# Fused attention and MLP layer: VectorE's exp tiles taken eight units ahead, more zero matmuls, and a one-quad first PV

## The chip, the cores and the metric

The kernel runs on one core of a Trainium2 chip. The metric is the device time of one execution in microseconds (us); lower is better. Each time here is a median of several executions. "Clock" is the mean granted clock of TensorE (PE) over an execution, 1.00 being full speed. ACT is ScalarE, DVE is VectorE.

## The reference, cut to what matters

```python
# x: (1, 2048, 640) bf16; 32 heads of 20; MLP width 1728
def _A_ref(x, wqkv, wo):
    q, k, v = ...                                   # split of x @ wqkv by head
    scores = jnp.einsum("bhqd,bhkd->bhqk", q, k) * (Dh ** -0.5)
    p = _softmax(scores, axis=-1)
    o = jnp.einsum("bhqk,bhkd->bhqd", p, v)
    return o.transpose(...).reshape(B, S, D) @ wo
h  = x + _A_ref(_layernorm(x), wqkv, wo)
h2 = h + _B_ref(_layernorm(h), w_gate, w_up, w_down)   # gelu(g) * u, then down
```

The attention has 32 x 2048 x 2048 exponentials. They are most of the work of this kernel.

## The kernel before

The kernel is written as a list of operations with priorities. A list scheduler inside the kernel, with its own table of durations, fixes each engine's program order when the kernel is built; the chip then runs these fixed orders with semaphores.

Words used below:

- A **tile** is 128 partitions by 512 columns of scores, for one head. The heads of a group of four are numbered j = 0 to 3, and head j's q and k lie in partitions 32j to 32j+31. Its score matmuls use only 32 rows of PE.
- A **unit** is three or two consecutive tiles; ACT takes their exp in one instruction of 1536 or 1024 columns. Units alternate between PSUM banks 0-2 and 3-4, so the scores of a unit can start when the exp two units earlier has freed its banks.
- A **group** (a "slot" in the code) is 64 tiles, about 22 units. Eight of its tiles (two in the first group) go to DVE, which computes exp in integer and bf16 arithmetic, two tiles at a time.
- **PV** multiplies finished probabilities with V, one **quad** (four heads) at a time. It frees the probability buffer, a ring of 18 tiles.
- The queries are handled in seven **chunks** (numbered 0 to 6, of 512, 512, 256, 256, 256, 128 and 128); output projection, LayerNorm and MLP of a finished chunk run as background work among the next chunk's attention. What is left of it after the last exp, with the last chunk's own part, is the **tail**.

How tiles are given out, before: DVE's tile is the next in the sequence after its unit, and its scores are issued right behind the unit's.

```python
        while i < len(tiles):                      # (cut)
            units.append(tiles[i:i + len(bs)])     # 3 or 2 tiles with consecutive j
            i += len(units[-1])
            want = min(nd, (k[0] - D_FIRST) * nd // D_SPAN + 1) if k[0] >= D_FIRST else 0
            if k[1] < want and tiles[i][0] == s_:
                dtile.append(tiles[i])             # the next tile: the next j
                i += 1                             # (cut)
```

```python
                return lambda eng: eng.matmul(out()[:, kk * nq:(kk + 1) * nq],       # scores, tile (s_, g, kb, j)
                                              kt_all[32 * j:32 * j + 32, g, kt * 128:(kt + 1) * 128],
                                              qt_all[32 * j:32 * j + 32, q0 // 512, g, q0 % 512:q0 % 512 + nq],
                                              start=True, stop=True, tile_position=(32 * j, 0), skip_group_check=True)
```

Padding: before it places a PV operation, the scheduler looks at how busy PE was in the last 3.4 us of its model, and adds groups of four zero matmuls (added to the output bank, so without effect) until a threshold is met. With nothing else to do, it places "warming" work (a full-size matmul, or a group of four zero ones) by a second threshold.

```python
                    while u < PAD_MIN * PAD_WIN and o.util < 1.1:
                        o.fns = o.fns + self.pad       # four zero matmuls, one per column group
                        o.dur += 0.215
```

## Time and profile before

The median is 928.82 us (three runs, 928.81 to 929.91).

| | read in | value |
|---|---|---|
| busy share of ACT | busy table | 95% |
| first exp starts, last exp ends | timeline of ACT | 35.74, 890.21 us |
| first to last exp ("the stream") | difference | 854.47 us |
| last exp to end ("the tail") | span less 890.21 | 37.15 us |
| exp of 1536 / 1024 columns, start to start | start times of the exps, median | 1.331 / 0.904 us |

The head of the page of the kernel before, with busy time and share by engine:

```profile
span 927.4 us, 23141 instructions
PE 837.1 (90%) x10069; PEld 356.9 (38%) x10126; DVE 811.3 (87%) x1703; ACT 883.2 (95%) x799; POOL 39.1 (4%) x117
```

Groups of the page: busy us and mean ns of one, then the engine's idle time ahead of them and what ended it. They are the scores, the two exp groups (ACT writes into either of two buffers) and the zero matmuls. Each exp group holds both widths, half of each, though its line names only 1536 columns.

```profile
L852 PE MATMUL ps<-qt_all,kt_all 32*128 32x256 bf16 (+2 forms) x3584 | 304.9, 289 | 51.2 <-ACT pts L339 29.1
L339 ACT ACTIVATE pts<-ps 128x1536 bf16<-128x1536 f32 x480 | 571.7, 1368 | 5.1 <-PE ps L852 3.8
L339 ACT ACTIVATE rege<-ps 128x1536 bf16<-128x1536 f32 x239 | 298.8, 1367 | 2.4 <-PE ps L339 1.5
L339 PE MATMUL ps<-kt_all,zer 128*32 128x512 bf16 x680 | 56.4, 384 | 0.0
```

ACT is idle only 7.5 us ahead of all 719 exps, and half of that is the first one. Note the 1368 ns: an exp is recorded longer than the mean spacing of exps, because successive records overlap. The Trainium skill ("Perfetto Trace Analysis", Per-instruction lifecycle) says that an ACT record runs on to the write's acknowledgement; this trace agrees, with 1.58 us recorded for 1536 columns against a spacing of 1.331. So the idle column misses delays shorter than the overlap, and I measure an exp's **delay** by start times: start to start, less the median of its width (1.331 or 0.904 us). Delays of at most 0.25 us I call **short**, the others **long** (pairs with a table load between them are left out). Before, the short ones sum to 6.6 us and the long ones to 7.0.

The tail in ACT's timeline (start, duration, group, and in brackets idle time and what ended it):

```profile
888.62 1.59 ACT L339 ACTIVATE rege<-ps 128x1536 bf16<-128x1536 f32 x1
890.23 1.28 ACT L339 ACT_TABLE_LOAD   x1
891.52 0.20 ACT L339 ACTIVATE nm<-off 128x1 f32<-128x1 f32 x1
896.02 0.70 ACT L567 ACTIVATE rege<-ps 128x640 bf16<-128x640 bf16 x1 [4.29 <-PE ps L561]
```

And PE's timeline there. The last scores are at 888.06; then come 25 down-projection matmuls of an older chunk (L1096), and the last PV starts at 891.89, 1.7 us after the last exp:

```profile
888.06 0.40 PE L852 MATMUL ps<-qt_all,kt_all 32*128 32x128 bf16 x12
888.39 3.57 PE L1096 MATMUL ps<-regw,rege 128*128 128x320 bf16 x25
891.89 0.45 PE L339 MATMUL ps<-pts,v_all 128*21 128x128 bf16 x17
```

### The profile page before, as it was taken

The page shows a single profiled execution, that of the slowest core. Times are in us where ns is not written, and L with a number is a line of the kernel's source. Part 1 is how long each engine was busy: PE and PEld are TensorE (multiplying, and loading weights), DVE is VectorE, ACT ScalarE, POOL GpSimd, SP SyncE. Part 2 cuts the span into 40 slices and gives each one's busy share as a digit, 9 for nine tenths or more (in the row PEclk, how much of TensorE's full clock was granted, in tenths as well). Part 3 has the DMA queues.
Part 4 walks back from the last instruction along what each step waited for, and adds up shares of the span by engine and source line. Part 5 has one row for each costly group of instructions (what it writes and reads, how often), then busy time and mean ns, then how long its engine had stood idle before and what let it go on. Part 6 is the DMA issues. An engine that isn't in the chain of part 4 may idle for free.

```text
span 927.4 us, 23141 instructions
## 1 busy us (share of the span) xinstructions
PE 837.1 (90%) x10069; PEld 356.9 (38%) x10126; DVE 811.3 (87%) x1703; ACT 883.2 (95%) x799; POOL 39.1 (4%) x117
## 2 busy tenths in 40 slices
PE   3998999899998998998797898999899998989998
PEld 2432322222232222233233333344345455546677
DVE  8859999999898998888798997988998997899972
ACT  6899999999999999999999999999999999999951
POOL 5000000000001000000001000000200200010100
PEclk9999999999999999999999999999999999999999
DMA  7301010322540000001021000011000100101000
GB/s 256 94 19 43 18 55 18 90 60 66 155 176 18 12 1 1 1 15 44 1 31 23 8 2 1 16 30 31 16 16 2 23 23 2 31 17 24 3 24 16
DMA packets 39517, 34.36 MB, mean 37 GB/s; under 512 B 19436, under 2 KB 36936, under 8 KB 39416
## 3 DMA queue, kind: packets, MB, share of 16 engines
q1 hardware_dynamic: 39416, 32.89, 12.7%
q8 instruction: 79, 1.29, 0.6%
q14 instruction: 22, 0.18, 0.1%
HBM read 20.12 MB, written 8.09 MB: 30 GB/s over the span
## 4 chain that ended last, share of the span: by engine, by line
ACT 73%; PE 14%; DVE 9%; DMA 2%; POOL 1%; issue 1%; SPq 0%
ACT pts L339 46%; ACT rege L339 25%; PE ps L1039 3%; PE ps L616 3%; DVE qt_all L339 3%; PE ps L1096 3%; PE ps L852 3%; PE ps L339 2%; DVE rege L339 2%; DMA regw<-in_A_wqkv_dram 1%; ACT L339 1%; DVE rege L812 1%; DVE qt_all L812 1%; POOL nw L339 0%; PE ps L561 0%
## 5 line engine op out<-in xcount | busy, mean ns | idle before, releaser
L339 ACT ACTIVATE pts<-ps 128x1536 bf16<-128x1536 f32 x480 | 571.7, 1368 | 5.1 <-PE ps L852 3.8
L852 PE MATMUL ps<-qt_all,kt_all 32*128 32x256 bf16 (+2 forms) x3584 | 304.9, 289 | 51.2 <-ACT pts L339 29.1
L339 ACT ACTIVATE rege<-ps 128x1536 bf16<-128x1536 f32 x239 | 298.8, 1367 | 2.4 <-PE ps L339 1.5
L852 PEld LDWEIGHTS ps<-qt_all,kt_all 32*128 32x128 bf16 x3584 | 96.4, 92 | 279.8 <-ACT pts L339 160.0
L339 DVE TENSOR_TENSOR qt_all<-qt_all 128x1024 bf16<-128x1024 bf16 (+1 forms) x240 | 164.4, 685 | 3.7
L1039 PE MATMUL ps<-rege,regw 128*128 128x256 bf16 (+2 forms) x957 | 149.2, 287 | 10.3 <-ACT rege L339 2.8
L339 PE MATMUL ps<-pts,v_all 128*21 128x256 bf16 (+2 forms) x2098 | 138.8, 290 | 1.0 <-DVE rege L339 1.0
L812 DVE TENSOR_SCALAR rege<-ps 128x512 int16<-128x512 f32 x154 | 105.3, 684 | 23.9 <-PE ps L852 23.1
L339 DVE TENSOR_SCALAR qt_all<-qt_all 128x1024 bf16<-128x1024 int16 (+1 forms) x288 | 115.8, 417 | 2.4
L339 PE MATMUL ps<-rege,v_all 128*21 128x256 bf16 (+2 forms) x1294 | 113.3, 292 | 0.1
L1039 PEld LDWEIGHTS ps<-rege,regw 128*128 128x128 bf16 x980 | 72.0, 97 | 65.4 <-issue 27.3
L616 PE MATMUL ps<-regw 128*128 128x512 bf16 (+1 forms) x342 | 82.1, 349 | 3.8 <-issue 1.3
L1096 PE MATMUL ps<-regw,rege 128*128 128x320 bf16 x448 | 78.7, 301 | 1.1 <-DVE rege L1064 0.5
L812 DVE TENSOR_SCALAR qt_all<-ps 128x512 int16<-128x512 f32 x96 | 65.6, 684 | 4.5 <-PE ps L852 3.6
L339 DVE TENSOR_SCALAR rege<-rege 128x1024 int16<-128x1024 int16 (+2 forms) x166 | 67.2, 421 | 1.3
L339 DVE TENSOR_TENSOR rege<-rege 128x1024 bf16<-128x1024 bf16 (+3 forms) x103 | 65.5, 644 | 0.9
L339 PEld LDWEIGHTS ps<-pts,v_all 128*21 128x21 bf16 x2098 | 50.2, 91 | 37.9 <-issue 31.7
L339 PE MATMUL ps<-kt_all,zer 128*32 128x512 bf16 x680 | 56.4, 384 | 0.0
L1085 DVE TENSOR_TENSOR rege<-rege,ps 128x512 bf16<-128x512 bf16 (+1 forms) x53 | 35.8, 677 | 16.4 <-PE ps L1039 16.4
L1096 PEld LDWEIGHTS ps<-regw,rege 128*128 128x128 bf16 x448 | 37.0, 97 | 32.7 <-issue 15.6
L339 PEld LDWEIGHTS ps<-rege,v_all 128*21 128x21 bf16 x1294 | 41.0, 91 | 20.6 <-issue 13.6
L616 PEld LDWEIGHTS ps<-regw 128*128 128x128 bf16 x360 | 28.6, 98 | 45.3 <-issue 20.9
(95 smaller groups left out, 575.3 us busy)
## 6 DMA issues: line engine op xcount, KB each, us to landing
rege<-in_A_x_dram SPq DMA_DIRECT2D x6, 640.0 KB, 5.2
q_rows<-regw SPq DMA_DIRECT2D x20, 128.0 KB, 1.7
out_dram<-rege SPq DMA_DIRECT2D x16, 160.0 KB, 2.0
regw<-in_B_w_gate_dram SPq DMA_DIRECT2D x1, 2160.0 KB, 13.3
regw<-in_B_w_up_dram SPq DMA_DIRECT2D x1, 2160.0 KB, 18.3
regw<-in_B_w_down_dram SPq DMA_DIRECT2D x1, 2080.0 KB, 23.4
kt_all<-k_rows SPq DMA_DIRECT2D x12, 160.0 KB
qt_all<-q_rows SPq DMA_DIRECT2D x12, 160.0 KB
```

Source lines behind the costliest of these rows:

```text
L339: return lambda eng: getattr(eng, method)(*args, **kwargs)
L616: yield op("pe", lambda eng, l=l, r=r, k=k: eng.matmul(bank(bk, n), l, r, start=(k == 0), stop=(k == len(steps) - 1)), c_mm(n), prio, mode ...
L812: d_ops.append(op("dve", lambda eng: eng.tensor_scalar(v[:, 512 * h:512 * h + 512], bank(b), EXP_MUL, -32000.0, ALU.mult, ALU.max), c_dve( ...
L852: return lambda eng: eng.matmul(out()[:, kk * nq:(kk + 1) * nq], kt_all[32 * j:32 * j + 32, g, kt * 128:(kt + 1) * 128], qt_all[32 * j:32 ...
L1039: op("pe", lambda eng, a=a, f=f, fi=fi: eng.matmul(bank(bk)[:, fi * nq:(fi + 1) * nq], w[:, a, F0[f]:F0[f] + 128], hnT[:, a, 128 * tb:128 ...
L1085: hdone.append(op("dve", lambda eng, bu=bu, fv=fv, w=w: eng.tensor_tensor(fv, fv, bank(bu, w), ALU.mult), c_dve(w), p, reads=[ku] + hkeys( ...
L1096: op("pe", lambda eng, f=f, o=o, hf=hf, bk=bk: eng.matmul(bank(bk, 320), ha_f[:, o:o + 128], wd[:, f, hf * 320:(hf + 1) * 320], start=(f = ...
```

## The change

The intent: DVE's tiles are spread over 20 units of a group in place of 16, and their scores are computed eight units ahead, across the border of a group, so that DVE never holds up the group's last PV. Padding thresholds go up, most at the end of a group. The first PV of a group takes one quad, not two. LayerNorm and output projection of a finished chunk get a priority above the rest of the background. The diff, cut to its core (the bookkeeping of tiles that belong to the next group, and a rewrite of `base` that gives the same values here, are left out):

```diff
-WARM_WIN, WARM_MIN = 3.4, 0.5
-PAD_WIN, PAD_MIN = 3.4, 0.42
+WARM_WIN, WARM_MIN = 3.4, 0.55
+PAD_WIN, PAD_MIN, PAD_END = 3.4, 0.5, 0.6
@@
-                    while u < PAD_MIN * PAD_WIN and o.util < 1.1:
+                    want = PAD_END if o.i in self.final else PAD_MIN
+                    while u < want * PAD_WIN and o.util < 1.1:
@@
-D_FIRST, D_SPAN = 1, 16
+D_FIRST, D_SPAN, D_LEAD, D_HOLD = 1, 20, 8, 4
-P_QK, P_PV, P_PRO, P_EPI, P_BG = 0, 1, 1.5, 2, 3
+P_QK, P_PV, P_PRO, P_EPI, P_LN, P_BG = 0, 1, 1.5, 2, 2.5, 3
@@
-                dtile.append(tiles[i])
+                dplan.append((len(units) - 1, tiles[i]))
@@
+        dtile = [None] * len(units)
+        u = 0
+        for n, x in dplan:
+            u = max(n - D_LEAD, u, D_FIRST, chunk_u[1] if slots[x[0]][0] == 1 else 0)
+            dtile[u] = x
+            u += 1
@@
-                if len(quads) < PV_QUADS and not final:
+                if len(quads) < PV_QUADS and not final and s_ in pv_bank:
@@ (D_HOLD: a finished DVE tile that waits four units or more past its lag gets a PV quad of its own)
+                if any(x[2][0] == s_ and u - x_unit[x[2]] >= D_LAG + D_HOLD for x in d_done):
@@
-            p = P_EPI if tail else P_BG
+            p = P_EPI if tail else P_LN
@@ (output projection: not before the residual's load)
-                                              for a in range(NA)], [("hnT", tt), "wo"], p))
+                                              for a in range(NA)], [("hnT", tt), "wo"], p, after=(sc.lw[("h", tt, hf)],)))
```

More of the change, by code (lines that the diff above doesn't have):

```diff
@@ L309 @@
 ND = 4
-D_PER_SLOT = (8, 8, 8, 8, 8, 8, 8)
+D_PER_SLOT = (8,) * len(SIZES)
 D_SLOT0 = 2
-D_FIRST, D_SPAN = 1, 16
+D_FIRST, D_SPAN, D_LEAD, D_HOLD = 1, 20, 8, 4
 RSQRT_MAGIC = float(0x5F3759DF)
-P_QK, P_PV, P_PRO, P_EPI, P_BG = 0, 1, 1.5, 2, 3
+P_QK, P_PV, P_PRO, P_EPI, P_LN, P_BG = 0, 1, 1.5, 2, 2.5, 3
 def bass_sequential_preLN__mha_block__glu_gated_geglu__prompt_kernel(
@@ L766, in bass_sequential_preLN__mha_block__glu_gated_geglu__prompt_kernel @@
         PAT = [((0, 1, 2), (3, 4))] * len(CHUNKS)
-        units, ubank, dtile, ends = [], [], [], []
+        units, ubank, dplan, ends = [], [], [], []
         i, in_slot = 0, {}
@@ L778, in bass_sequential_preLN__mha_block__glu_gated_geglu__prompt_kernel @@
             want = min(nd, (k[0] - D_FIRST) * nd // D_SPAN + 1) if k[0] >= D_FIRST else 0
-            if k[1] < want and tiles[i][0] == s_:
-                dtile.append(tiles[i])
+            if k[1] < want and i < len(tiles) and tiles[i][0] == s_:
+                dplan.append((len(units) - 1, tiles[i]))
                 k[1] += 1
                 i += 1
-            else:
-                dtile.append(None)
             k[0] += 1
@@ L787, in bass_sequential_preLN__mha_block__glu_gated_geglu__prompt_kernel @@
         assert all(k[1] % 2 == 0 for k in in_slot.values())
+        chunk_u = [min(u for u, tl in enumerate(units) if slots[tl[0][0]][0] == c) for c in range(len(CHUNKS))]
+        dtile = [None] * len(units)
[4 more added lines that the diff above has]
+            u += 1
         d_tiles = set(x for x in dtile if x)
@@ L907, in unit @@
                     for x in list(d_done):
-                        if u - x_unit[x[2]] >= D_LAG and x[2][3] not in [y[2][3] for y in have]:
+                        if u - x_unit[x[2]] >= D_LAG and x[2][0] == s_ and x[2][3] not in [y[2][3] for y in have]:
                             have.append(x)
                             d_done.remove(x)
-                while final and d_done:
+                if any(x[2][0] == s_ and u - x_unit[x[2]] >= D_LAG + D_HOLD for x in d_done):
                     have = []
                     for x in list(d_done):
-                        if x[2][3] not in [y[2][3] for y in have]:
+                        if x[2][0] == s_ and u - x_unit[x[2]] >= D_LAG and x[2][3] not in [y[2][3] for y in have]:
+                            have.append(x)
+                            d_done.remove(x)
+                    quads.append(have)
+                while final and any(x[2][0] == s_ for x in d_done):
+                    have = []
+                    for x in list(d_done):
+                        if x[2][0] == s_ and x[2][3] not in [y[2][3] for y in have]:
                             have.append(x)
@@ L936, in unit @@
                     sc.final.add(pv)
-                    assert not d_done and not d_raw
+                    assert not any(x[0] == s_ for x in d_raw)
                     epilogue(s_, bk)
@@ L942, in base @@
             n = CHUNKS[c][1]
-            if n == 128:
-                return 2 + (c == len(CHUNKS) - 1)
-            return 2 * (c % 2) if n < 512 else 0
+            if n == 512:
+                return 0
+            half = sum(1 for _, m in CHUNKS[:c] if m == 256) % 2
+            return 2 * half + (n == 128 and CHUNKS[c - 1][1] == 128)
         def epilogue(s_, bk):
```

## The prediction

> **What bounds it now.** ScalarE: the page's busy table gives ACT 883.2 us of 927.4 (95%); the chain of work that ended last is 73% ACT. In ACT's timeline the first exp starts at 35.74 us and the last ends at 890.21; in between, ACT's waits sum to about 3 us. Start to start, an exp of 1536 columns takes 1.331 us, one of 1024 columns 0.904 us (medians); all that the 719 exps lose over these adds up to about 14 us. So: 36 us of head, 854 us of saturated ACT stream, 37 us of tail. The Trainium skill ("Perfetto Trace Analysis", Identifying the Most-Contended Engine) says to improve the engine with the highest occupancy; the trace agrees that it is ACT, and the change takes no work from it.
>
> **What the change does** (order of the built programs):
> - The same 719 exps in the same shapes; the same count on VectorE. No tile moves from ACT to VectorE, only its place.
> - 268 more zero matmuls on PE (67 groups of four at about 0.22 us: some 14 us, an estimate), and 5 more full-size ones.
> - The head is unchanged until well after the first exp.
> - LayerNorm and output projection of a finished chunk get a higher priority, so the later chunks' MLP comes earlier. After the last scores the kernel before still has 56 down matmuls of chunk 4, all 140 gate/up and 28 down of chunk 5, then the last chunk. The changed one has 89 gate/up and 28 down of chunk 5, then the last chunk.
> - ACT has one more table load (1.28 us); chunk 5's gelu (1.69 us) stands right behind the last exp, where ACT idled 4.29 us before.
>
> **Padding** pays only if PE falls to half clock. The Trainium skill ("TensorE: Matmul & The Clock Gate", Part 1) describes a gate that halves the clock after an idle window. Here the granted clock is 1.00 in every stretch after 19.8 us, so more padding has nothing to win; it takes PE slots that are mostly free. I expect the 854 us stream to change by -5 to +4 us; earlier VectorE tiles and the single first quad may remove a few waits (longest: 1.46 us).
>
> **The tail holds the gain.** Before: the last exp ends at 890.21; PE is in 25 down matmuls until 891.9, so the final PV starts 1.6 us late; the last LayerNorm is through at 904.3; then PE works until 924.6, on 70 up and 28 down of chunk 5 (4.0 + 4.0 us) and on the last chunk. After: final PV with the last exp (-1.4); 70 up and 5 down fit into the LayerNorm chain's gaps (-4.0, -0.7); table load and gelu delay one copy by about 0.3. Sum -6.5 us: tail 37.2 to about 30.5.
>
> **Prediction.** 928.8 - 6.5 - 1 = 921.3 us; 8 in 10 between 915.5 and 926.5. Faster by over 2% 0.03, within 2% 0.96, slower by over 2% 0.01.
>
> **What would show it.** First to last exp still about 854 us at pitches 1.331 and 0.904; granted clock 1.00 in both; last exp to end about 30.5 us; chunk 5's gelu right after the last exp; busy time of zero matmuls up by 40%, the span not.
>
> **What would make it wrong.** Zero groups ahead of scores making ACT wait, above all at group ends (stream longer by over 5 us); earlier VectorE tiles holding banks or VectorE's queue; or most of the 14 us of lost pitch going away.

## The result, and the profile after

The changed kernel takes 928.59 us (median of four runs, 927.72 to 930.35), against 929.37 for the kernel before in the same comparison. Ratios here are the mean time of one kernel's fast runs over that of the other's of the same rounds, so not quite the ratio of the medians: 0.9989, 95% interval 0.9964 to 1.0013. That is no difference, and 928.6 lies outside the predicted 915.5 to 926.5.

The page of the changed kernel, the lines that answer to those of before:

```profile
span 926.2 us, 23729 instructions
PE 877.4 (95%) x10399; PEld 371.0 (40%) x10399; DVE 816.0 (88%) x1703; ACT 888.4 (96%) x800; POOL 37.5 (4%) x117
```

```profile
L858 PE MATMUL ps<-qt_all,kt_all 32*128 32x256 bf16 (+2 forms) x3584 | 334.2, 288 | 18.6 <-ACT pts L340 8.3
L340 ACT ACTIVATE pts<-ps 128x1536 bf16<-128x1536 f32 x480 | 564.7, 1301 | 6.7 <-PE ps L858 4.2
L340 ACT ACTIVATE rege<-ps 128x1536 bf16<-128x1536 f32 x239 | 290.3, 1299 | 3.9 <-PE ps L340 2.5
L340 PE MATMUL ps<-kt_all,zer 128*32 128x512 bf16 x948 | 77.9, 384 | 0.0
```

The timeline of ACT from the last exp on:

```profile
895.22 1.45 ACT L340 ACTIVATE rege<-ps 128x1536 bf16<-128x1536 f32 x1
896.69 1.28 ACT L340 ACT_TABLE_LOAD   x1
897.98 1.70 ACT L340 ACTIVATE rege<-rege 128x1792 bf16<-128x1792 bf16 x1
901.10 0.69 ACT L568 ACTIVATE rege<-ps 128x640 bf16<-128x640 bf16 x1
```

Three things are to be seen.

1. **The tail got shorter as predicted.** The last exp now ends at 896.67 and the span at 926.21: 29.5 us in place of 37.2. Chunk 5's gelu (1.70 us at 897.98) stands right behind the last exp.
2. **The stream got longer.** First to last exp (35.21 to 896.67) takes 861.46 us in place of 854.47. The 7.0 us eat the 7.6 us of the tail. The median spacings are still 1.331 and 0.904 us; short delays sum to 12.3 us (6.6 before), long ones to 8.4 (7.0).
3. **The same scores keep PE busy longer.** 3584 score matmuls in both, mean 289 and 288 ns, yet 334.2 us busy in place of 304.9. Busy time counts overlapped records once, so the same records overlap less. PE's idle time ahead of the scores falls from 51.2 to 18.6 us: they find PE busy more often. And an exp's mean record shrinks from 1368 to 1300 ns, though ACT got no faster: the median spacings are the same, so successive records overlap less. Why they do is not shown.

The third point shows directly in PE's timeline. In the kernel before, a unit of three tiles and DVE's tile, four score matmuls, take 0.39 us together; a single one of 512 columns has a record of 0.38 to 0.39 us too:

```profile
361.58 0.39 PE L852 MATMUL ps<-qt_all,kt_all 32*128 32x512 bf16 x4
```

In the changed kernel, three score matmuls, a unit of two and DVE's tile, take 0.60 us:

```profile
365.56 0.60 PE L858 MATMUL ps<-qt_all,kt_all 32*128 32x512 bf16 x3
```

### The profile page after: what moved, and what is told of

Read it like the earlier page. It is cut to its first block, busy times and chain, and to the rows that moved or that the text cites. A ratio compares the mean times of both kernels' runs of the same rounds, so it can differ in the third digit from the quotient of the medians.

```text
span 926.2 us, 23729 instructions
## 1 busy us (share of the span) xinstructions
PE 877.4 (95%) x10399; PEld 371.0 (40%) x10399; DVE 816.0 (88%) x1703; ACT 888.4 (96%) x800; POOL 37.5 (4%) x117
## 4 chain that ended last, share of the span: by engine, by line
ACT 59%; PE 29%; DVE 10%; DMA 2%; issue 0%; SPq 0%
ACT pts L340 38%; ACT rege L340 20%; PE ps L858 9%; PE ps L1110 6%; PE ps L1053 5%; PE ps L340 5%; DVE qt_all L340 3%; PE ps L617 3%; DVE rege L340 3%; DMA regw<-in_A_wqkv_dram 1%; DVE rege L818 1%; ACT L340 1%; DVE qt_all L818 1%; PE ps L562 0%; PE ps L976 0%
## 5 line engine op out<-in xcount | busy, mean ns | idle before, releaser
L340 ACT ACTIVATE pts<-ps 128x1536 bf16<-128x1536 f32 x480 | 564.7, 1301 | 6.7 <-PE ps L858 4.2
L858 PE MATMUL ps<-qt_all,kt_all 32*128 32x256 bf16 (+2 forms) x3584 | 334.2, 288 | 18.6 <-ACT pts L340 8.3
L340 ACT ACTIVATE rege<-ps 128x1536 bf16<-128x1536 f32 x239 | 290.3, 1299 | 3.9 <-PE ps L340 2.5
L858 PEld LDWEIGHTS ps<-qt_all,kt_all 32*128 32x128 bf16 x3584 | 110.9, 92 | 244.7 <-ACT pts L340 118.9
L1053 PE MATMUL ps<-rege,regw 128*128 128x256 bf16 (+2 forms) x980 | 156.3, 290 | 7.1 <-ACT rege L340 5.4
L340 PE MATMUL ps<-pts,v_all 128*21 128x256 bf16 (+2 forms) x2098 | 140.9, 290 | 0.0
L818 DVE TENSOR_SCALAR rege<-ps 128x512 int16<-128x512 f32 x154 | 105.5, 686 | 32.2 <-PE ps L858 30.9
L340 DVE TENSOR_SCALAR qt_all<-qt_all 128x1024 bf16<-128x1024 int16 (+1 forms) x288 | 118.6, 417 | 3.4
L1053 PEld LDWEIGHTS ps<-rege,regw 128*128 128x128 bf16 x980 | 73.1, 98 | 66.9 <-issue 30.6
L617 PE MATMUL ps<-regw 128*128 128x512 bf16 (+1 forms) x360 | 86.4, 350 | 0.7 <-DMA regw<-in_A_wqkv_dram 0.5
L340 PE MATMUL ps<-kt_all,zer 128*32 128x512 bf16 x948 | 77.9, 384 | 0.0
L818 DVE TENSOR_SCALAR qt_all<-ps 128x512 int16<-128x512 f32 x96 | 65.8, 686 | 13.1 <-PE ps L858 12.3
L340 PEld LDWEIGHTS ps<-pts,v_all 128*21 128x21 bf16 x2098 | 50.2, 91 | 44.6 <-issue 33.7
L340 PEld LDWEIGHTS ps<-rege,v_all 128*21 128x21 bf16 x1294 | 39.1, 91 | 23.5 <-issue 16.9
```

The source lines that it names most:

```text
L340: return lambda eng: getattr(eng, method)(*args, **kwargs)
L617: yield op("pe", lambda eng, l=l, r=r, k=k: eng.matmul(bank(bk, n), l, r, start=(k == 0), stop=(k == len(steps) - 1)), c_mm(n), prio, mode ...
L818: d_ops.append(op("dve", lambda eng: eng.tensor_scalar(v[:, 512 * h:512 * h + 512], bank(b), EXP_MUL, -32000.0, ALU.mult, ALU.max), c_dve( ...
L1053: op("pe", lambda eng, a=a, f=f, fi=fi: eng.matmul(bank(bk)[:, fi * nq:(fi + 1) * nq], w[:, a, F0[f]:F0[f] + 128], hnT[:, a, 128 * tb:128 ...
```

## The experiments

**Theories.** *Padding*: more zero matmuls stand in front of scores. *Lead*: computing DVE's tiles early hurts by itself, through PSUM banks, DVE's queue or the border of groups. *Priority*: background work got in the way. Later, from the lines above, *row groups*. The Trainium skill ("TensorEngine Tiling (Array Packing)", Tiling Modes, Key Properties) says: "Tiles operate independently: Different tiles can execute LdWeights and Matmul in parallel". Two score matmuls of the same row group don't run in parallel (the 0.60 us above). In the kernel before, a unit has j = a, a+1 (and a+2), and DVE's tile is the next one, so it never shares its unit's row groups. With a lead of eight, the unit it rides with is 20 ACT tiles and about three DVE tiles earlier. The last tile of that unit then lies 24 places before DVE's tile, a multiple of four, and so has its j. Counted from the kernels' lists, 0 of 250 DVE tiles **collide** with their unit before, and 243 after.

The two traces show this on more than one pair. Their score matmuls can be matched, in order, to the kernels' lists. Take the DVE tiles of the chunks of 512 queries whose matmul comes right behind their unit's on PE. In the changed kernel all 74 that collide start 0.18 us or more after the unit's last matmul, 226 ns in the median. In the kernel before the median of 79 is 4 ns, and 63 of them start within 50 ns.

Results at a glance; more below. "Scores" is PE's busy time on score matmuls, "short" and "long" are the summed delays, all in us from the profiled run; the clock is the lowest of that kernel's runs. The expectations give the score time by another count (252 and 280 us for what is 304.9 and 334.2 here), so only its differences can be compared.

| run | collide | median | ratio | scores | stream | short | long | tail | clock |
|---|---|---|---|---|---|---|---|---|---|
| before | 0 | 928.82 | 1 | 304.9 | 854.5 | 6.6 | 7.0 | 37.2 | 0.995 |
| changed | 243 | 928.59 | 0.9989 | 334.2 | 861.5 | 12.3 | 8.4 | 29.5 | 0.998 |
| old_padding | 243 | 931.77 | 1.0028 | 336.2 | 861.2 | 11.7 | 8.9 | 30.0 | 0.987 |
| new_padding_alone | 0 | 934.35 | 1.0050 | 304.6 | 860.2 | 7.1 | 12.2 | 37.5 | 0.998 |
| old_order_of_tiles | 0 | 930.69 | 1.0004 | 309.5 | 857.5 | 7.1 | 9.5 | 34.9 | 1.000 |
| old_priority | 243 | 936.89 | 1.0073 | 333.5 | 862.1 | 12.8 | 8.5 | 37.1 | 0.998 |
| before_one_unit_earlier | 249 | 936.96 | 1.0063 | 337.1 | 863.3 | 11.7 | 11.0 | 38.4 | 0.994 |
| changed_lead6_no_collision | 0 | 932.79 | 1.0019 | 307.9 | 863.5 | 6.8 | 15.7 | 31.7 | 0.996 |
| changed_lead6 | 96 | 925.89 | 0.9949 | 319.1 | 857.8 | 7.8 | 9.0 | 30.3 | 0.998 |
| priority_alone | 0 | 927.35 | 0.9963 | 303.4 | 853.8 | 6.4 | 6.6 | 36.1 | 0.998 |
| no_lead_old_padding | 0 | 944.75 | 1.0149 | 303.0 | 874.1 | 5.2 | 28.0 | 33.7 | 0.996 |
| no_lead_new_padding | 0 | 942.81 | 1.0130 | 301.8 | 872.7 | 5.3 | 26.6 | 32.2 | 1.000 |
| changed_old_first_pv | 243 | 938.18 | 1.0083 | 337.6 | 868.5 | 11.9 | 16.3 | 31.8 | 0.991 |
| changed_no_padding | 243 | 982.53 | 1.0536 | 371.9 | 916.1 | 12.5 | 62.9 | 30.0 | 0.878 |
| lead11_no_collision | 0 | 925.55 | 0.9966 | 316.9 | 858.0 | 8.2 | 9.2 | 31.4 | 0.998 |
| lead11_no_collision_old_padding | 0 | 930.77 | 1.0020 | 320.3 | 860.0 | 9.1 | 10.3 | 31.5 | 0.993 |
| spread16_lead6_no_collision | 0 | 922.01 | 0.9921 | 312.1 | 853.8 | 8.0 | 4.7 | 30.7 | 1.000 |
| near8_no_collision | 0 | 942.32 | 1.0147 | 313.5 | 871.8 | 7.0 | 23.7 | 30.6 | 0.993 |
| spread16_lead6 | 206 | 934.06 | 1.0053 | 333.3 | 861.3 | 11.9 | 9.0 | 34.7 | 0.995 |
| spread16_lead6_no_collision_old_padding | 0 | 929.26 | 0.9988 | 311.9 | 857.5 | 7.7 | 8.5 | 35.3 | 0.996 |

All outputs are right. Ratios are to runs of the kernel before on the same chip (medians 929.4 to 930.2 in these comparisons).

### First: one part of the change at a time

**old_padding**: the changed kernel with

```diff
-WARM_WIN, WARM_MIN = 3.4, 0.55
-PAD_WIN, PAD_MIN, PAD_END = 3.4, 0.5, 0.6
+WARM_WIN, WARM_MIN = 3.4, 0.5
+PAD_WIN, PAD_MIN, PAD_END = 3.4, 0.42, 0.42
```

> The changed kernel with the old padding thresholds (0.42 and 0.50 of the window, nothing extra at group ends): 744 zero matmuls in place of 948. Padding theory (zero groups use up PE's slack, and the scores behind them make ACT wait): first to last exp back from 861.5 to about 855 us, tail still about 29.5, so about 921.5 us, 0.8% faster than before. Theory of the earlier VectorE tiles, or of the new priority: the stream stays at about 861 and the time at about 928.

The stream stayed at 861.2 us with 204 zero matmuls fewer. The padding theory of the longer stream falls. But another thing came up: five of its six runs had a clock under 1.00, and the time follows it, from 928.15 us at 1.000 to 938.82 at 0.987. The profiled run was the one at 1.000; in the traces of other kernels with a clock under 1.00, each spell is 3.41 us, or a multiple, at half clock. So 0.013 of 936.8 us is 12.2 us of lost clock, or about seven such windows that lose half of 3.41 us each. The run took 10.7 us more: some 1.5 us for each window (an estimate from these numbers).

**new_padding_alone**: the kernel before with the three new thresholds and the two new lines of padding of the diff above.

> The kernel before with the new padding thresholds alone: 876 zero matmuls in place of 680, tail work as before (254 gate/up and 112 down matmuls after the last scores). Padding theory: stream of exps 854.5 grows by 5 to 7 us, tail 37, so about 934 us. The other theories: stream within 2 us of 854.5, about 929 us.

Here the padding does cost: 0.5%, a stream of 860.2, and the loss is in the long delays (12.2 against 7.0), not in the short ones. One window of 3.4 us at half clock lies in the profiled run, but four of the six runs at clock 1.000 took 933.7 to 934.5 too.

**old_order_of_tiles**: the changed kernel with

```diff
-D_FIRST, D_SPAN, D_LEAD, D_HOLD = 1, 20, 8, 4
+D_FIRST, D_SPAN, D_LEAD, D_HOLD = 1, 16, 0, 99
```

> The changed kernel with VectorE's tiles back where they were (no lead, spread over 16 units, no forced flush); new padding, priority and PV rule kept: 884 zero matmuls. Theory of the earlier tiles (they put scores and PV where they collide): stream back to about 855, tail about 31, so about 922 us. Padding theory: stream about 860, so about 928 us.

The stream fell to 857.5 us, the short delays to 7.1, and PE's time on scores from 334 to 309.5: 4.0 of the 7.0 us are in the place of the tiles (lead, spread and hold, which this edit resets together). The tail came out at 34.9, not 31, so the total gained nothing.

**old_priority**: the changed kernel with the priority of the background again.

```diff
-P_QK, P_PV, P_PRO, P_EPI, P_LN, P_BG = 0, 1, 1.5, 2, 2.5, 3
+P_QK, P_PV, P_PRO, P_EPI, P_LN, P_BG = 0, 1, 1.5, 2, 3, 3
```

> The changed kernel with LayerNorm and output projection of a finished chunk back at background priority: 280 gate/up and 82 down matmuls are left after the last scores, in place of 229 and 56. My account of the tail: the tail grows from 29.5 back to about 34.5 us. If the new priority also causes the longer stream (background work cut smaller, projections waiting at PE's head), the stream falls to about 855 and the total is about 926; if not, the stream stays at about 861 and the total is about 933.

The tail went back to 37.1 us (I expected 34.5), and the stream stayed (862.1). So the new priority, together with the rest, is worth 7.5 us of tail, and it is not what made the stream longer.

### Second: row groups or lead

**before_one_unit_earlier**: the kernel before (rebuilt from the changed source with old padding, old priority, old PV rule; with a lead of 0 that build has the instruction counts of the kernel before) with a lead of one unit:

```diff
-D_FIRST, D_SPAN, D_LEAD, D_HOLD = 1, 16, 0, 99
+D_FIRST, D_SPAN, D_LEAD, D_HOLD = 1, 16, 1, 99
```

> The kernel before with one thing changed: each VectorE tile's scores ride with the unit of scores just ahead of their old one. In the kernel before none of the 250 such tiles shares a 32-row group of PE with the unit it rides with; here 249 do (counted from the kernel's lists), in the changed kernel 243 do. Row-group theory (a colliding tile's scores no longer run beside its unit's but after them, about 0.2 us of PE each on most of 250): PE's time on score matmuls between first and last exp grows from about 252 to about 280 us as it did in the changed kernel, and the stream of exps grows from 854.5 to 858 or more, total about 933. Rival (it is the early use of PSUM banks and of VectorE, or the crossing of group ends, that hurts, not the row groups): one unit of lead changes nearly nothing, score matmuls stay at about 252 us, total about 930.

One unit of lead did the damage alone. The groups of the scores and of one kind of exp in its page:

```profile
L858 PE MATMUL ps<-qt_all,kt_all 32*128 32x256 bf16 (+2 forms) x3584 | 337.1, 290 | 28.8 <-ACT pts L340 16.2
L340 ACT ACTIVATE pts<-ps 128x1536 bf16<-128x1536 f32 x480 | 565.3, 1303 | 12.3 <-PE ps L858 11.2
```

Scores 337.1 us and exps of 1303 ns, as in the changed kernel; short delays 11.7 us. Its profiled run had a clock of 0.995: 10.2 us at half clock, from 797 us on, around which 4.0 of its 11.0 us of long delays lie. Its three runs at a clock of 1.000 took 935.1, 935.3 and 936.2, still 5 us or more over the kernel before. The rival would have had 930.

**changed_lead6_no_collision**: the changed kernel with a lead of six and a push to the next free row group.

```diff
-D_FIRST, D_SPAN, D_LEAD, D_HOLD = 1, 20, 8, 4
+D_FIRST, D_SPAN, D_LEAD, D_HOLD = 1, 20, 6, 4
@@
             u = max(n - D_LEAD, u, D_FIRST, chunk_u[1] if slots[x[0]][0] == 1 else 0)
+            while x[3] in [y[3] for y in units[u]]:
+                u += 1
+            assert u <= n + 1
             dtile[u] = x
```

> The changed kernel with a lead of six units, and each VectorE tile pushed on to the next unit that leaves its row group free: 0 of 250 collide; padding, priority and PV rule as in the change; 237 gate/up and 56 down matmuls left after the last scores. Row-group theory: score matmuls about 252 us, stream about 857, tail about 30, so 922 to 925 us, faster than both kernels. Rival (lead itself hurts): score matmuls not much below 280 us or, if they are, stream still about 861 and total about 928.

This missed. The scores' time (307.9 us) and the short delays (6.8) did what the row-group theory says, but the stream was 863.5, because the long delays doubled to 15.7. So the stream has a second cause of delay, and this version traded one for the other. ACT's waits show where the long ones are (us in total, times, longest us): exps that wait for a PV to free their probability buffer.

```profile
ACT pts L340 <- PE ps L340: 7.3, 7, 1.5
ACT rege L340 <- PE ps L340: 3.7, 3, 2.2
```

**changed_lead6**: the same without the push.

```diff
-D_FIRST, D_SPAN, D_LEAD, D_HOLD = 1, 20, 8, 4
+D_FIRST, D_SPAN, D_LEAD, D_HOLD = 1, 20, 6, 4
```

> The changed kernel with a lead of six units and no regard to row groups: 96 of 250 collide. Row-group theory: score matmuls between the two, about 263 us, stream about 859, tail about 30. Rival: the same as with a lead of eight.

As the row-group theory says, between the two in score time (319.1 us); stream 857.8. It holds both kinds of tile in one kernel: those that come right behind their unit, in the chunks of 512 queries, start 220 ns after it in the median where they collide (31 tiles) and 3 ns where they don't (50). Its short delays, 7.8 us, are no more than those of some versions without collisions (up to 9.1), so 96 collisions don't show in that sum. It is half a per cent faster than the kernel before (0.9949), and some 0.4% faster than the changed one (0.9989), which ran in another comparison.

**priority_alone**: the kernel before with the new priority alone.

```diff
-P_QK, P_PV, P_PRO, P_EPI, P_BG = 0, 1, 1.5, 2, 3
+P_QK, P_PV, P_PRO, P_EPI, P_LN, P_BG = 0, 1, 1.5, 2, 2.5, 3
@@
-            p = P_EPI if tail else P_BG
+            p = P_EPI if tail else P_LN
@@ (and the output projection's wait for the residual, as in the change)
```

> The kernel before with the new priority of LayerNorm and output projection alone: 280 gate/up and 80 down matmuls left after the last scores, in place of 280 and 109. Fewer by 29 down matmuls at 0.142 us: tail shorter by up to 4 us, stream unchanged at about 854.5, total about 926; the full tail gain of the change (7.6 us) needs the other parts as well. If the priority does nothing without them: 930.

The stream is unchanged at 853.8, and the total is 0.4% better. The tail gained 1.0 us of the up to 4 that I expected.

### Third: the other parts, and candidates

**no_lead_new_padding** is the changed kernel with the first edit below, **no_lead_old_padding** with both:

```diff
-D_FIRST, D_SPAN, D_LEAD, D_HOLD = 1, 20, 8, 4
+D_FIRST, D_SPAN, D_LEAD, D_HOLD = 1, 20, 0, 4
@@
-WARM_WIN, WARM_MIN = 3.4, 0.55
-PAD_WIN, PAD_MIN, PAD_END = 3.4, 0.5, 0.6
+WARM_WIN, WARM_MIN = 3.4, 0.5
+PAD_WIN, PAD_MIN, PAD_END = 3.4, 0.42, 0.42
```

> A candidate: the changed kernel with no lead (tiles spread over 20 units as in the change, each riding with the unit it follows in the sequence: 0 of 250 collide) and the old padding thresholds (604 zero matmuls); priority and PV rule as in the change; 260 gate/up and 63 down matmuls left after the last scores. Row-group account: delays under 0.25 us per exp sum to about 7 us in place of 12.3, stream about 855 if the long delays stay at 7 us; tail about 33; total 923 to 926 at full clock. If the stream stays at 861, row groups aren't what made it long.

> The same with the padding of the change (788 zero matmuls). Row-group account: small delays about 7 us as well; tail about 33. The padding cost the kernel before 5 us of long delays; if that holds here, stream about 860 and total about 929; if padding costs only where the order happens to be bad, about 925.

Both missed by far, at 944.8 and 942.8 us, though their short delays are the smallest of all (5.2 and 5.3). The long delays are 28.0 and 26.6 us; 20.1 of the 26.6 are waits for PV. With tiles spread over 20 of 22 units and no lead, the last DVE tile rides two units before the group's end. So in these versions the spread needs the lead; whether late tiles are the reason is taken up below. Padding made little difference to the long delays here.

**changed_old_first_pv**: the changed kernel with the old rule.

```diff
-                if len(quads) < PV_QUADS and not final and s_ in pv_bank:
+                if len(quads) < PV_QUADS and not final:
```

> The changed kernel with the old rule for the first PV of a group (two quads at once); all else as in the change, 243 of 250 collide, 260 gate/up and 62 down matmuls left. If the single first quad bought shorter waits for PV, the long delays (8.4 us in the changed kernel) grow by 2 us or more and the total goes to 931 or more; if it matters little, the total is 928 to 931, from a tail about 1.5 us longer.

938.2 us, but every run had a clock of 0.991 to 0.998, and the profiled one has 10.2 us at half clock just where 5 us of its extra long delays lie (100 to 150 us). At the same clock of 0.998 the two kernels took 934.2 and 930.4 us, one run each. So the single first quad seems to help; how much of that is a shorter wait and how much is the clock is not separated.

**changed_no_padding**: no zero and no warming matmuls.

```diff
-WARM_WIN, WARM_MIN = 3.4, 0.55
-PAD_WIN, PAD_MIN, PAD_END = 3.4, 0.5, 0.6
+WARM_WIN, WARM_MIN = 3.4, 0.0
+PAD_WIN, PAD_MIN, PAD_END = 3.4, 0.0, 0.0
```

> The changed kernel with no zero and no warming matmuls at all. My prediction said padding has nothing to win at a granted clock of 1.00; with less padding five of six runs of the changed kernel fell to 0.998 to 0.987. If padding is what holds the clock, it falls well under 0.98 here and the time goes over 940; if not, the clock stays at 0.99 or more and the stream gets shorter by some us.

Its page, the granted clock in tenths over 40 slices, beside the busy share of PE:

```profile
span 981.2 us, 21654 instructions
PE   4998988889888998998898998999999989798988
PEclk9997879699676799997576598999999999869899
```

PE is above 80% busy in nearly every slice and yet spends a quarter of the span at half clock: 0.878 on average, 982.5 us. Padding holds the clock of this order. And PE need not be wholly idle to lose it: in the 3.41 us before each of the 18 spells at half clock, PE's records fill 45 to 76% of the time.

### Fourth: is lateness the cause of the long waits, and a better version

Three of these have the push to a free row group, as above, and these sizes: **lead11_no_collision** the first, **lead11_no_collision_old_padding** the first and the old thresholds, **spread16_lead6_no_collision** the second.

```diff
-D_FIRST, D_SPAN, D_LEAD, D_HOLD = 1, 20, 8, 4
+D_FIRST, D_SPAN, D_LEAD, D_HOLD = 1, 20, 11, 4
```

```diff
-D_FIRST, D_SPAN, D_LEAD, D_HOLD = 1, 20, 8, 4
+D_FIRST, D_SPAN, D_LEAD, D_HOLD = 1, 16, 6, 4
```

**near8_no_collision** takes the nearest free unit, earlier or later, around a lead of eight:

```diff
-            dtile[u] = x
-            u += 1
+            lo = 0 if not d_seen else d_seen[-1] + 1
+            lo = max(lo, D_FIRST, chunk_u[1] if slots[x[0]][0] == 1 else 0)
+            ok = [v for v in range(lo, n + 1) if x[3] not in [y[3] for y in units[v]]]
+            u = min(ok, key=lambda v: (abs(v - u), v))
+            d_seen.append(u)
+            dtile[u] = x
+            u += 1
```

> The changed kernel with a lead of eleven units, each VectorE tile pushed on to the next unit that leaves its row group free (0 of 250 collide; 9.8 units of lead on average; the last tile of a group rides 13 units before the group's end, in the median, in place of 10); padding, priority and PV rule of the change; 241 gate/up and 56 down matmuls left. Two-cause account (collisions make short delays, late tiles make long waits for PV): short delays about 7 us, long ones about 8, stream about 856, tail about 30, total 921 to 924. If the long waits come from the moved order as such and not from late tiles: long delays 12 us or more, total over 927.

> The same with the old padding thresholds: 640 zero matmuls in place of 928, 232 gate/up and 56 down matmuls left. Two-cause account: the same stream of about 856 in a run at clock 1.00, total 921 to 924; with PE idle more often I expect the clock to fall to 0.998 or less in some runs, which then are 1.5 us longer for each 3.4 us at half clock.

> As the version with a lead of six and no collision (5 units from the last tile to the group's end, long delays 15.7 us), but the tiles planned over 16 units of a group in place of 20: the last tile rides 10 units before the end. Late tiles as the cause of the long waits: long delays fall to 9 us or less, short ones stay at 7, stream about 857, tail about 30.5 (261 gate/up, 56 down left), total about 924. If lateness is not the cause: long delays about 15 again, about 931.

> The changed kernel with a lead of about eight, each tile set to the nearest unit, earlier or later, that leaves its row group free (0 collide, 7.2 units of lead on average, the last tile 9 units before the group's end): only the collisions differ from the change. 260 gate/up and 56 down left, 1052 zero matmuls. Two-cause account: short delays from 12.3 to about 7, long ones about 8.5 as in the change, stream about 856, tail about 30.5, total 922 to 925.

spread16_lead6_no_collision is the best version: 922.01 us, ratio 0.9921 (0.9909 to 0.9934), all five runs at a clock of 1.000. It has the stream of the kernel before (853.8 us) with nearly the tail of the changed one (30.7 us). Its page:

```profile
L861 PE MATMUL ps<-qt_all,kt_all 32*128 32x256 bf16 (+2 forms) x3584 | 312.1, 289 | 32.5 <-ACT pts L340 17.7
L340 ACT ACTIVATE pts<-ps 128x1536 bf16<-128x1536 f32 x480 | 571.3, 1369 | 6.1 <-PE ps L861 4.3
```

```profile
ACT pts L340 <- PE ps L340: 1.6, 3, 1.0
ACT rege L340 <- PE ps L340: 0.3, 1, 0.3
```

Scores 312.1 us, exps back at 1369 ns, waits for PV 1.9 us where the version spread over 20 units had 11.0. Its last tile rides 10 units before the group's end in place of 5. That fits lateness. But the kernel before, with its last tile only 6 units before the end, has just 7.0 us of long delays, and near8_no_collision refutes lateness as the only cause: its last tile rides 9 units before the end, and yet it has 23.7 us of long delays, 15.5 of them waits for PV:

```profile
ACT pts L340 <- PE ps L340: 8.4, 8, 2.5
ACT rege L340 <- PE ps L340: 7.1, 4, 2.8
```

What puts these PVs late in its program order stays open. The lead of eleven came out at 925.6, a little above its range, with 9.2 us of long delays; with the old thresholds its clock fell to 0.993 to 0.998 in all runs, and its time to 930.8.

The last two runs edit the best version.

**spread16_lead6** takes the push out (which also puts its last tile 12 units before the group's end, not 10); **spread16_lead6_no_collision_old_padding** keeps it and sets the old thresholds.

```diff
-            while x[3] in [y[3] for y in units[u]]:
-                u += 1
-            assert u <= n + 1
```

```diff
-WARM_WIN, WARM_MIN = 3.4, 0.55
-PAD_WIN, PAD_MIN, PAD_END = 3.4, 0.5, 0.6
+WARM_WIN, WARM_MIN = 3.4, 0.5
+PAD_WIN, PAD_MIN, PAD_END = 3.4, 0.42, 0.42
```

> The best version so far (tiles planned over 16 units, lead of six; 922.0 us) without the push to a free row group: 206 of 250 tiles collide in place of none. Row-group account: PE's time on scores from 258 to about 275 us, short delays from 8.0 to about 12 us, stream at least 4 us longer; total 927 or more (the tail has 84 down matmuls left in place of 56, some 3 us more of it). If the row groups hardly matter, the short delays stay at 8 us.

> The best version so far with the old padding thresholds (800 zero matmuls in place of 944; 266 gate/up and 84 down matmuls left in place of 261 and 56). As in the two earlier pairs I expect the clock to leave 1.00 in most runs (0.998 to 0.990) and the total to be 926 or more, of which some 3 us are the longer tail; if it keeps 1.00 with a stream of about 854, padding isn't needed in this version.

With collisions back, scores take 333.3 us, short delays 11.9, and the stream is 7.5 us longer, of which 3.9 are short delays and 4.3 long ones. With the old thresholds the clock left 1.000 in two of four runs, and the time is 7.3 us longer; 4.5 of that is a longer tail in the profiled run (more background work was left). The two runs at 1.000 took 928.1 and 928.8 us, so the share of the clock is small here.

## Why the prediction was wrong, point by point

- **"ScalarE bounds it; 36 + 854 + 37 us"**: right. Every result above is read from these three parts.
- **"The tail holds the gain: -6.5 us, to about 30.5"**: right. Measured 37.15 to 29.54, -7.6 us. The last PV starts as the last exp ends, and chunk 5's gelu stands behind it. But the priority doesn't do it alone: with it alone the tail is 36.1, with all but it 37.1, and with the old places of the tiles 34.9.
- **"No tile moves from ACT to VectorE, only its place"**: this is the step that failed. The place was costed at nothing (a gain of about 1 us, with -5 to +4 for the whole stream); the stream measured +7.0. The place decides which row group is free. 243 of 250 tiles met their own row group, and PE spent 29.3 us more on the same matmuls (0.12 us for each colliding tile, as an average; lead11_no_collision has 12 us more without a collision, so not all of it need be theirs). Of the 7.0 us, 5.7 are short delays and 1.4 long ones (they needn't add up exactly: pairs at table loads are left out). The short part is shown: in all 12 kernels without collisions that were profiled, the kernel before among them, short delays sum to 5.2 to 9.1 us, and in the seven with 206 or more collisions to 11.7 to 12.8 (changed_lead6, with 96, has 7.8); one unit of lead in the kernel before was enough to move it from one set to the other, and the push to a free row group moved the best version the other way.
- **"It takes PE slots that are mostly free"**: right for the changed kernel's stream (861.2 with 744 zero matmuls, 861.5 with 948), wrong for the kernel before (+5.7 us, in long delays; a part of it may be that run's one window at half clock).
- **"More padding has nothing to win"**: wrong. I read a clock of 1.00 in one run of the kernel before and took it as a property. In other rounds the kernel before itself fell to 0.995, and the changed kernel without any padding has 0.878 (the kernel before was not run without). The changed order with the old thresholds took 931.8 us in the median, 3 us more, with clocks down to 0.987. The Trainium skill ("TensorE: Matmul & The Clock Gate", Part 1) describes the window of 3.4 us; the runs agree, with spells of 3413 ns at a clock of 0.5. I used that page's idle window as a reason against padding, without asking how near to the edge the new order would come.
- **"What would make it wrong"** named zero groups ahead of scores, banks and VectorE's queue. The first was refuted by a run; row groups were not on the list.

What stays open: why particular orders have long delays (4.7 to 28 us in the padded versions), of which waits for PV are a large part where they were looked up. Late DVE tiles fit the versions without lead or with 20 units and a lead of six, but not near8_no_collision, and no run shows that they are the cause. And no run makes or takes away collisions with every tile left in its unit: each of these edits moves tiles by a unit or more, and with them the order of the program.

## What to carry to other kernels

When matmuls are packed into parts of the array, an instruction's neighbours are part of its cost: before moving one, count which part its new neighbours use. On a saturated engine, sum start-to-start times, not idle times: here the loss was in delays of 0.1 us that hide under overlapping records, and an exp's mean record getting shorter went with it. A full clock in one run doesn't show that its padding is spare: take it away, or look at several runs.

## What the Trainium skill lacked or had wrong

- "TensorEngine Tiling (Array Packing)" says that different tiles run in parallel, and gives no cost for two matmuls in the same row group. Here a tile of 512 columns right behind a unit that holds its row group started 226 ns after it (median of 74), and 4 ns after it where the row group was free (79).
- "Perfetto Trace Analysis" (Optimization Strategy) advises to look for gaps between slices, and doesn't say there that overlapping records hide delays. ACT's records overlap (1.58 us recorded, 1.331 us apart), so within the stream gaps show 3.8 us (7.5 less the first exp's) where the start times show 13.6 us of delays.
- "TensorE: Matmul & The Clock Gate" gives one idle window as the condition for half clock (Part 1), and further down frequent short idle times as another, but not how much idle time in a window is enough. In the changed kernel without padding PE was busy for 90% of the span, and for 45 to 76% of the 3.41 us before each spell, and its clock still averaged 0.878. No run here gives the limit either.
